# Loading half of w1 ahead of x, and a new order for the opening of a fused convolution and max-out kernel

## The chip, the cores and the metric

The kernel runs on one core of a Trainium2 chip. A core has five engines that run side by side, each in the order of its own instruction list: TensorE (PE in the profile; its weight loads stand apart as PEld), VectorE (DVE), ScalarE (ACT), GpSimd (POOL) and SyncE (SP, which here only starts transfers). They wait for each other by semaphores. The metric is device time of one execution in microseconds. Three runs of the kernel before took 405.36, 405.75 and 405.82 us; the median is 405.75.

## The reference

Two stages. First a convolution whose weights are a softmax of an input: for every token, head and tap (8 heads, 7 taps), `w = softmax(weight_gen)` over the taps, and the output is the sum over the 7 latest tokens of `w * x`. Then a max-out layer on all 33280 tokens of width 192:

```
h1 = x @ w1        # 192 x 1024
h2 = x @ w2
out = maximum(h1, h2) @ w_out   # 1024 x 192
```

## The kernel before

**The algebra.** `max(h1, h2) = h1 + relu(h2 - h1)`, so the kernel needs `wd = w2 - w1` (bf16) for the hidden products, a relu, `w_out`, and a small product `w10 = w1 @ w_out` that gives the `h1` part straight from the convolved x. `wd` has six blocks of 512 features: blocks 0 and 1 are the first 128 rows of w2 - w1 for the two halves of the features, block 2 the last 64 rows of both halves; blocks 3, 4 and 5 are the same with the two halves of the partitions swapped, made on PE with a shifted identity (`turn`, into `turned` in PSUM) and copied out by ACT (`turn_out`).

**The tiling.** Tokens lie as 128 partitions by 260 columns. Columns come in batches of 16, a batch in units: four of 4 columns in the first two batches (units 0 to 7), 8 columns from then on. A unit's path: ACT takes exp of the weights (`exp_sum`, line 153), DVE sums over the taps (`red`, line 168), ACT takes the log (`ln`, line 172), DVE subtracts it (`shift`, line 177), ACT takes exp again into `en_t` (`weights`, line 191), DVE multiplies with seven shifted copies of x into `m_t` (`mul`, line 211). In units 0 to 7 PE sums the taps and transposes in one go with identity products (`sum_transpose`, line 281), and ACT copies the sum out (`sums_out`, line 293); from unit 8 on DVE adds the taps (lines 227 to 236) and a transposing DMA on SP brings the result to `yt`. Then PE makes the hidden tiles (line 336), ACT the relus (line 346), PE the output products (lines 376 and 388), ACT copies the results out (`evac`, line 434) and SP stores them.

**What sets the order.** The opening, to about 47 us, is a list of steps written out by hand, `OPENING` (line 721). Each step is a letter and its numbers; the program emits the steps' instructions one after the other, so that each engine gets its own share of them in this order. An `@step` behind a load makes its trigger wait for the end of that other step. The letters:

```
lg.b  load the weights of batch b (SP for b < 2, else POOL)    xf  load the first columns of x (SP)
lw.h.w  load half h of the first 128 rows of w1 (w=0) or w2 (w=1)   lt.h.w  half h of the last 64 rows
lx.b.o.n  load n columns of x in bf16 (POOL)   lo  load w_out (POOL)   lh  copy the halo
xa, xv  cast x on ACT, on DVE    X exp   n sum over taps   l log   s subtract   W exp into en_t   m multiply
c.i  cast block i of w1 (ACT)   d.i  block i of wd (DVE)   t.i  turn it (PE)   T.i  copy the turned block (ACT)
v, V  transpose w1 on PE, copy it (ACT)   p, C  product w10 (PE), copy it (ACT)   k.n  n idle products that keep PE busy
y, e  sum and transpose (PE), copy it (ACT)   h hidden tile (PE)   r relu (ACT)
A, B, D  first and second half of the output products (PE; B is a wait on ACT)   E  copy the results (ACT)
```

The loads of SP use eight semaphores in turn, so that the ninth load waits for the landing of the first, the tenth for the second, and so on. After the opening a loop over groups of three hidden tiles runs to the end; the softmax steps of later batches stand at fixed places in it (`SOFTMAX_AT`, line 744), in ACT's list. The last result of all is copied from two PSUM banks by one ACT instruction into `o_last` and stored by two transfers, one from ACT's queue and one from SP's (line 422).

Of the kernel before, what the change touches and what calls it, by code (L numbers as in the profile page):

```python
# [17 lines left out]
def _sub(base: bass.AP, off: int, dims):  # L18
    ap = [list(base.ap[0])] + [[int(s), int(c)] for s, c in dims]
    return dataclasses.replace(base, offset=base.offset + off, ap=ap)  # L20
# [3 lines left out]
def kernel(  # L24
# [9 lines left out]
    nc = tc.nc  # L34

    B, S, D = x.shape
# [17 lines left out]
    def dcol(c):  # L54

        return (c + ROT) % CPP
# [292 lines left out]
    def column(c):  # L349

        for u, (b, o, n) in enumerate(UNITS):
            k = c - BATCHES[b][0] - o
            if 0 <= k < n:
                return u, k // 2, k % 2

    def place(p):

        u, i, _ = column(2 * p)
        b, o, n = UNITS[u]
        return BATCHES[b][0] + o + i, n // 2  # L360
# [55 lines left out]
    def evac(p, n):  # L416

        tile_, at = op_at[p]
        o = o_t[0]
        if p == NT // 2 - 1:  # L420

            nc.scalar.copy(out=_sub(o_last, 0, [[D, 2], [1, D]]),
                           in_=_sub(tile_, at, [[512, 2], [1, D]]))
            for j, eng in enumerate((nc.scalar, nc.sync)):
                eng.dma_start(
                    out=bass.AP(tensor=out.tensor, offset=dcol(place(p)[0] + 2 * j) * D, ap=[[CPP * D, P], [1, D]]),
                    in_=o_last[:, j * D:(j + 1) * D],
                )
            return
        runs = [[q for q in range(p, p + n) if column(2 * q)[0] == u]  # L430
                for u in range(column(2 * p)[0], column(2 * (p + n - 1))[0] + 1)]
        for qs in runs:
            c, h = place(qs[0])
            copied = nc.scalar.copy(out=_sub(o, c % 24 * D, [[D, len(qs)], [h * D, 2], [1, D]]),  # L434
                           in_=_sub(tile_, at + (qs[0] - p) * D, [[D, len(qs)], [512, 2], [1, D]]))
        stores = []
        for q in range(p, p + n):
            u, i, _ = column(2 * q)
            if u == NU - 2 and UNITS[u][2] == 8 and i % 2:
                stores.append((nc.sync, place(q)[0] - 1, [4 * D, 2], [1, 2 * D]))  # L440
            elif u < NU - 1 and i == UNITS[u][2] // 2 - 1:
                w = i + 1
                for k in range(0, 2 * w, w if u in PARTED else 2 * w):
                    stores.append((nc.sync, place(q)[0] - i + k, [1, (w if u in PARTED else 2 * w) * D]))
            if u == NU - 1:
                stores.append((nc.sync, place(q)[0], [2 * D, 2], [1, D]))
        for eng, c, *ap in stores:

            def issue(eng=eng, c=c, ap=ap, o=o):
                eng.dma_start(  # L450
                    out=bass.AP(tensor=out.tensor, offset=dcol(c) * D, ap=[[CPP * D, P], *ap]),
                    in_=_sub(o, c % 24 * D, ap),
                )

            if 3 <= u < NU - 3:
                held.append(issue)
            else:
                while u > 3 and held:
                    held.pop(0)()
                issue()  # L460
        return copied
# [8 lines left out]
    OUTS, c = [[], [], []], 0  # L470
    for g in range(3, len(GROUPS)):
        most = 4 if g == 3 else 2 if GROUPS[g][1] == 2 or len(OUTS[-1]) == 4 else 4
        n = min(most, ready[g] - c)
# [21 lines left out]
    def hidden(g, now=(), between=lambda: None, beside=lambda: None, ahead=lambda: None,  # L495
               before=lambda: None, after=lambda: None):


        t0, n = GROUPS[g]
        rd = room(g)  # L500
        for t in range(t0, t0 + n - 1):
            hid_tile(t)
        if now:
            out_room(now, "a" if n == 1 and "a" in ps else None)
            last = out_first(now)
        for t in range(t0, t0 + n - 1):
            relu(rd, t, 1)
        go = relay(last) if now else None
        hid_tile(t0 + n - 1)
        before()  # L510
        if len(now) > 2:
            beside()
        relu(rd, t0 + n - 1, 1)
        ahead()
        if now:
            out_second(now, go)
            evac(now[0] // 2, len(now) // 2)
        between()
        after()
        if len(now) <= 2:  # L520
            beside()

    def rest_of_results(c):

        parts = [p for p in (c[:4], c[4:-2], c[-2:]) if p]
        assert max(map(len, parts)) <= 4
        go = []
        for i, now in enumerate(parts):
            out_room(now, ("r", "a", "c")[i])
            go.append(relay(out_first(now)))  # L530
            if i:
                out_second(parts[i - 1], go[i - 1])
                evac(parts[i - 1][0] // 2, len(parts[i - 1]) // 2)
        out_second(parts[-1], go[-1])
        evac(parts[-1][0] // 2, len(parts[-1]) // 2)
# [10 lines left out]
    o_last = consts.tile([P, 2 * D], FP32, name="o_last")  # L546
# [155 lines left out]
    def results_buffer(_):  # L702
# [16 lines left out]
    }  # L719

    OPENING = """
        lg.0 xf.-6.6 xf.0.4 lt.1.0 lt.0.0 k.2 lw.0.1 k.19 lw.0.0 lt.1.1 lw.1.0 lt.0.1 X.0.0.2 k.1 n.0.0.2
        X.0.1.2 lw.1.1 k.1 k.2 n.0.1.2 l.0.0.2 s.0.0.2 xa.-6.4 l.0.1.2 W.0.0.0 lx.0.4.4@l.0.0.2 lg.1 xv.-2.6
        W.0.0.1 s.0.1.2 W.0.12 c.0 lx.0.12.4@W.0.12 W.0.8 m.0.0.0 m.0.0.1 W.0.4 y.0.0 y.0.1 c.2 e.0.0 c.1
        e.0.1 d.0 d.2 t.0 k.3 t.2 T.3 d.1 T.4 h.0 h.1 t.1 X.1 r.0 lx.0.8.4 T.1 lo.0 r.1 m.0.4 n.1 v.0 h.2
        lx.1.0.8 V.1 y.1 r.2 l.1 h.3 e.1 m.0.8 lg.2@l.1 s.1 V.0 m.0.12 r.3 h.4 W.1.0 m.1.0 y.2 h.5 r.4 p.0
        e.2 r.5 h.6 lx.1.8.8@r.4 lg.3@e.2 y.3 W.1.8 h.7 lh.2 C.1 C.0 C.2 A.3 W.1.4 X.2 r.6 e.3 B.3 m.1.4 h.8
        D.3 y.4 r.7 r.8 Z.0 E.3 n.2 X.3 l.2 m.1.8 A.4 e.4 W.1.12 lx.2.0.8.0@r.7 B.4 h.9 D.4 h.10 r.9 E.4 s.2
        r.10 lg.4@r.9 y.5 W.2.0 A.5 h.11 B.5 h.12 e.5 D.5 n.3 r.11 r.12 A.6 m.1.12 E.5 h.13 B.6 D.6 y.6 r.13
        E.6 h.14 e.6 l.3 lx.2.8.8@r.13 h.15 r.14 A.7 W.2.8 B.7 y.7 D.7 r.15 e.7 E.7  # L730
    """

    make_identity(nc, ident_f)
# [91 lines left out]
```

## Time and profile before

| | |
|---|---|
| median of 3 runs | 405.75 us |
| the profiled execution | 405.37 us, of which the span is 403.6 us |
| PE busy | 394.8 us, 98% of the span |
| DVE busy | 369.1 us, 91% |
| ACT busy | 360.9 us, 89% |
| DMA | 63.16 MB moved, mean 157 GB/s |
| granted TensorE clock | 1.00 throughout |

The span runs from the first instruction of the program to the last; the 1.8 us between it and the execution's time lie around it. In the timeline a row has the start and the length in microseconds, then engine, line, operation, and what it writes and reads. A stretch in which nothing on the longest chain runs is shown as "issue". The landing of a transfer is given in the views of a tile as the time from its issue to its landing.

### The profile page before, as it was taken

The numbers are of one execution on the slowest core, as the hardware profiler recorded it, in microseconds if no ns is written. First come the engines' busy times: TensorE is split into PE (matmuls) and PEld (weight loads), VectorE is DVE, ScalarE is ACT, GpSimd is POOL, SyncE is SP. The second block draws the span as 40 slices with busy tenths as digits, with TensorE's granted clock in tenths as the row PEclk, the third lists the DMA queues.
The fourth block names the chain that finished last, engine by engine and source line by source line (L and its number), as shares of the span: only waits on it lengthen the run. The fifth ranks groups of instructions, "written<-read, shape, count | busy, mean of one in ns | idle before, by whom it ended". The sixth has DMA issues, their size and how long they took to land.

```text
span 403.6 us, 16321 instructions
## 1 busy us (share of the span) xinstructions
PE 394.8 (98%) x7499; PEld 321.3 (80%) x7499; DVE 369.1 (91%) x211; ACT 360.9 (89%) x466; POOL 72.3 (18%) x96
## 2 busy tenths in 40 slices
PE   7799999999999999999999999999999999999996
PEld 3589999777778777778777778877777877787996
DVE  5999999999999999999999999999999999998200
ACT  5999899999999989999899999989999899888872
POOL 3111031211122210222220122122012121200000
PEclk9999999999999999999999999999999999999999
DMA  8956468767768646864766667777457847558304
GB/s 262 222 140 151 120 124 167 183 164 133 190 110 222 182 79 129 240 187 80 217 187 107 141 192 193 99 215 198 81 115 228 178 80 200 141 106 193 104 31 169
DMA packets 60883, 63.16 MB, mean 157 GB/s; under 512 B 47641, under 2 KB 48665, under 8 KB 60816
## 3 DMA queue, kind: packets, MB, share of 16 engines
q1 hardware_dynamic: 52816, 40.15, 36.4%
q0 software_dynamic: 7856, 21.89, 27.4%
q8 instruction: 58, 0.95, 1.0%
q10 hardware_dynamic: 144, 0.10, 0.1%
q14 instruction: 9, 0.07, 0.1%
HBM read 36.55 MB, written 25.56 MB: 154 GB/s over the span
## 4 chain that ended last, share of the span: by engine, by line
PE 92%; ACT 5%; DMA 1%; SPq 1%; issue 0%
PE op_ps L376 42%; PE hdc L336 13%; PE hdb L336 13%; PE hda L336 13%; PE op_ps L388 8%; ACT rd_t L346 2%; DMA ws0E<-in_moe_w_dram 1%; PE hdp L336 1%; PE yps L281 1%; ACT en_t L191 1%; ACT yt L293 1%; ACT e_t L153 0%; ACT w1t L644 0%; SPq L574 0%; ACT w L622 0%
## 5 line engine op out<-in xcount | busy, mean ns | idle before, releaser
L376 PE MATMUL op_ps<-wo,rd_t 64*128 64x192 bf16 x4160 | 210.6, 243 | 0.0
L376 PEld LDWEIGHTS <-rd_t 64*128 64x128 bf16 x4160 | 181.0, 94 | 14.7
L211 DVE TENSOR_TENSOR m_t<-xb,en_t 128x10752 bf16<-128x10752 bf16 (+2 forms) x39 | 187.8, 4821 | 1.5 <-ACT en_t L191 1.4
L336 PEld LDWEIGHTS <-wd 64*128 64x128 bf16 x1824 | 96.8, 94 | 40.4 <-issue 2.5
L346 ACT ACTIVATE rd_t<-hdc 128x1024 bf16<-128x1024 f32 x82 | 84.1, 1025 | 17.8 <-PE hdc L336 16.2
L253 POOL CAST gate<-yt 128x1 f32<-128x1 bf16 x30 | 39.9, 1332 | 271.3 <-DMA yt<-y_t 271.3
L346 ACT ACTIVATE rd_t<-hda 128x1024 bf16<-128x1024 f32 x81 | 83.4, 1030 | 0.2 <-ACT o_t L434 0.2
L346 ACT ACTIVATE rd_t<-hdb 128x1024 bf16<-128x1024 f32 x81 | 83.5, 1031 | 0.0
L227 DVE TENSOR_TENSOR m_t<-m_t 128x4608 bf16<-128x4608 bf16 (+1 forms) x30 | 73.0, 2433 | 0.1
L336 PE MATMUL hdc<-yt,wd 64*128 64x512 bf16 (+1 forms) x552 | 67.9, 353 | 0.0
L434 ACT COPY o_t<-op_ps 128x384 f32<-128x384 f32 (+1 forms) x99 | 56.1, 577 | 12.4 <-PE op_ps L376 12.3
L336 PE MATMUL hdb<-yt,wd 64*128 64x512 bf16 (+1 forms) x540 | 67.1, 355 | 0.0
L336 PE MATMUL hda<-yt,wd 64*128 64x512 bf16 (+1 forms) x540 | 67.1, 355 | 0.0
L388 PE MATMUL op_ps<-w,yt 64*128 64x192 bf16 x780 | 55.5, 243 | 0.0
L388 PEld LDWEIGHTS <-yt 64*128 64x128 bf16 x780 | 39.0, 94 | 14.5 <-issue 0.3
L233 DVE TENSOR_TENSOR m_t<-m_t 128x3072 bf16<-128x3072 bf16 (+1 forms) x30 | 50.2, 1674 | 0.1
L191 ACT ACTIVATE en_t<-wg_t 128x896 bf16<-128x896 f32 (+3 forms) x48 | 35.7, 773 | 3.0 <-PE op_ps L376 2.0
L236 DVE TENSOR_TENSOR y_t<-m_t 128x1536 bf16<-128x1536 bf16 (+1 forms) x30 | 27.5, 916 | 0.6
L177 DVE TENSOR_TENSOR wg_t<-wg_t,sum_t 128x280 f32<-128x280 f32 (+6 forms) x46 | 22.2, 483 | 0.0
L168 DVE TENSOR_REDUCE sum_t<-e_t 128x64 f32<-128x448 f32 (+3 forms) x31 | 19.7, 639 | 2.3 <-ACT e_t L153 2.3
L125 POOL DMA_DIRECT2D xb<-in_x_dram x34 | 18.2, 537 | 17.3 <-ACT rd_t L346 11.0
L153 ACT ACTIVATE e_t<-wg_t 128x896 f32<-128x896 f32 (+2 forms) x18 | 15.9, 886 | 2.1 <-DMA wg_t<-in_weight_gen_dram 2.1
(40 smaller groups left out, 110.0 us busy)
## 6 DMA issues: line engine op xcount, KB each, us to landing
out_dram<-o_t SPq DMA_DIRECT2D x21, 768.0 KB, 4.3
xb<-in_x_dram POOLq DMA_DIRECT2D x30, 384.0 KB, 5.0
out_dram<-o_t SPq DMA_DIRECT2D x22, 384.0 KB, 3.7
wg_t<-in_weight_gen_dram POOLq DMA_DIRECT2D x13, 448.0 KB, 5.7
xb<-xb POOLq DMA_DIRECT2D x7, 288.0 KB, 5.1
wg_t<-in_weight_gen_dram SPq DMA_DIRECT2D x2, 448.0 KB, 5.2
xb<-in_x_dram POOLq DMA_DIRECT2D x4, 192.0 KB, 6.4
xs<-in_x_dram SPq DMA_DIRECT2D x1, 576.0 KB, 4.3
```

The costliest lines, as they stand in the source:

```text
L177: nc.vector.tensor_tensor(out=w_t, in0=w_t, in1=_sub(s_ts[b], hs.start, [[1, hs.stop - hs.start], [0, K]]), op=ALU.subtract)
L191: act = nc.scalar.activation(out=_sub(en_ts[b], (o * WGC + ((i or 0) * J + j) * N * K) * 2, [[2 * N, K], [2, N], [1, 2]]), in_=_sub(wg_ts[ ...
L211: return nc.vector.tensor_tensor(out=m_out, in0=x_in, in1=_sub(en_ts[b], at * H * 2, [[2, K * n * H], [0, G // 2], [1, 2]]), op=ALU.mult,)
L227: nc.vector.tensor_tensor(out=taps(0, 1, 3), in0=taps(0, 1, 3), in1=taps(3, 1, 3), op=ALU.add)
L233: nc.vector.tensor_tensor(out=taps(0, 2, 2), in0=taps(0, 2, 2), in1=taps(1, 5, 2), op=ALU.add)
L236: nc.vector.tensor_tensor(out=_sub(y_ts[b], o * D, [[64, 2], [P, 3 * w // 2], [1, 64]]), in0=taps(0, 1, 1), in1=taps(2, 1, 1), op=ALU.add,)
L253: nc.gpsimd.tensor_copy(out=gate, in_=yt[:, 0:1])
L336: nc.tensor.matmul(hid_out(t, f, j), lhsT=wd_at(j, s, f // 4, f % 4 * P, P), rhs=_sub(yt_ts[u][half(j), :], (s + j) % 3 * P, [[3 * P, w // ...
L346: relu_of[t0] = nc.scalar.activation(out=rd[:, k * 1024:(k + n) * 1024], in_=hd[:, at:at + n * 1024], func=AF.Relu)
L376: return nc.tensor.matmul(op_out(c), lhsT=rd[rows, k * 1024 + at:k * 1024 + at + P], rhs=wo[rows, f * D:(f + 1) * D], start=False, stop=(r ...
L388: nc.tensor.matmul(op_out(c + j), lhsT=yt_ts[u][half(j), (3 * i + (s + j) % 3) * P:(3 * i + (s + j) % 3 + 1) * P], rhs=w10[half(j), s * D: ...
L434: copied = nc.scalar.copy(out=_sub(o, c % 24 * D, [[D, len(qs)], [h * D, 2], [1, D]]), in_=_sub(tile_, at + (qs[0] - p) * D, [[D, len(qs)] ...
```

## The change

Three things change; the rest of the program is the same, and every step of the opening is still there.

1. The list `OPENING` is written in another order. On SP's queue the first half of the first 128 rows of w1 (`lw.0.0`) is loaded ahead of x instead of sixth in the weights; the last rows (`lt`) come ahead of the second halves; the first rows of w2 come last before `lg.1`. On DVE both `n`, then both `s`, come ahead of the cast of x, and `d.2` ahead of `d.0`. On ACT both `l` come ahead of `xa`, `c.0` right behind it, `W.0.8` and `W.0.4` ahead of `W.0.0.1`, and the order of the casts, copies and relus differs up to `e.7`. On PE all but one of the 28 idle products stand ahead of the first `y` (25 before), and `t.1` comes ahead of `h.0` instead of behind `h.1`.
2. Some triggers wait for other steps: `lx.0.4.4` for `l.0.1.2`, `lx.0.12.4` for nothing of its own, `lx.0.8.4` for `W.0.12`, `lo` for `e.0.0`, `lg.3` for `r.3` (and it now stands ahead of `lx.1.8.8`, which waits for `W.1.0`).
3. The last copy is split: ACT copies the one half of `o_last`, DVE the other, each followed by its store. In the built program DVE's copy waits for the semaphore of ACT's copy.

```diff
@@ -419,9 +419,8 @@
-            nc.scalar.copy(out=_sub(o_last, 0, [[D, 2], [1, D]]),
-                           in_=_sub(tile_, at, [[512, 2], [1, D]]))
-            for j, eng in enumerate((nc.scalar, nc.sync)):
+            for j, (eng, copy) in enumerate(((nc.scalar, nc.scalar.copy), (nc.sync, nc.vector.tensor_copy))):
+                copy(out=o_last[:, j * D:(j + 1) * D], in_=tile_[:, at + 512 * j:at + 512 * j + D])
                 eng.dma_start(
@@ -719,15 +718,15 @@
     OPENING = """
-        lg.0 xf.-6.6 xf.0.4 lt.1.0 lt.0.0 k.2 lw.0.1 k.19 lw.0.0 lt.1.1 lw.1.0 lt.0.1 X.0.0.2 k.1 n.0.0.2
-        X.0.1.2 lw.1.1 k.1 k.2 n.0.1.2 l.0.0.2 s.0.0.2 xa.-6.4 l.0.1.2 W.0.0.0 lx.0.4.4@l.0.0.2 lg.1 xv.-2.6
-        W.0.0.1 s.0.1.2 W.0.12 c.0 lx.0.12.4@W.0.12 W.0.8 m.0.0.0 m.0.0.1 W.0.4 y.0.0 y.0.1 c.2 e.0.0 c.1
-        e.0.1 d.0 d.2 t.0 k.3 t.2 T.3 d.1 T.4 h.0 h.1 t.1 X.1 r.0 lx.0.8.4 T.1 lo.0 r.1 m.0.4 n.1 v.0 h.2
-        lx.1.0.8 V.1 y.1 r.2 l.1 h.3 e.1 m.0.8 lg.2@l.1 s.1 V.0 m.0.12 r.3 h.4 W.1.0 m.1.0 y.2 h.5 r.4 p.0
-        e.2 r.5 h.6 lx.1.8.8@r.4 lg.3@e.2 y.3 W.1.8 h.7 lh.2 C.1 C.0 C.2 A.3 W.1.4 X.2 r.6 e.3 B.3 m.1.4 h.8
-        D.3 y.4 r.7 r.8 Z.0 E.3 n.2 X.3 l.2 m.1.8 A.4 e.4 W.1.12 lx.2.0.8.0@r.7 B.4 h.9 D.4 h.10 r.9 E.4 s.2
-        r.10 lg.4@r.9 y.5 W.2.0 A.5 h.11 B.5 h.12 e.5 D.5 n.3 r.11 r.12 A.6 m.1.12 E.5 h.13 B.6 D.6 y.6 r.13
-        E.6 h.14 e.6 l.3 lx.2.8.8@r.13 h.15 r.14 A.7 W.2.8 B.7 y.7 D.7 r.15 e.7 E.7
+        lg.0 lw.0.0 xf.-6.6 xf.0.4 X.0.0.2 n.0.0.2 lt.1.1 lt.1.0 lt.0.0 X.0.1.2 lw.1.0 lt.0.1 n.0.1.2
+        l.0.1.2 l.0.0.2 k.2 s.0.1.2 xa.-6.4 lw.0.1 s.0.0.2 c.0 lw.1.1 k.3 lx.0.4.4@l.0.1.2 lg.1 W.0.0.0
+        xv.-2.6 W.0.8 W.0.4 W.0.0.1 k.1 W.0.12 lx.0.12.4 m.0.0.0 k.19 m.0.0.1 k.2 d.2 y.0.0 y.0.1 d.0 c.1
+        t.0 lx.0.8.4@W.0.12 e.0.0 e.0.1 lo.0@e.0.0 t.2 c.2 T.4 k.1 T.3 d.1 t.1 h.0 h.1 X.1 r.0 T.1 h.2 m.0.4
+        y.1 n.1 m.0.8 v.0 r.1 l.1 r.2 e.1 lx.1.0.8 V.1 s.1 V.0 m.0.12 h.3 r.3 h.4 lg.2@l.1 W.1.0 m.1.0 y.2
+        h.5 lg.3@r.3 p.0 r.4 r.5 h.6 lx.1.8.8@W.1.0 h.7 lh.2 e.2 C.0 W.1.4 C.2 C.1 y.3 r.6 A.3 W.1.8 m.1.4
+        X.2 B.3 h.8 e.3 D.3 y.4 W.1.12 Z.0 r.7 E.3 r.8 A.4 h.9 X.3 m.1.8 n.2 lx.2.0.8.0@W.1.12 B.4 e.4 l.2
+        h.10 D.4 s.2 lg.4@l.2 y.5 r.9 E.4 A.5 h.11 r.10 B.5 D.5 e.5 r.11 h.12 W.2.0 n.3 m.1.12 A.6 E.5 h.13
+        B.6 D.6 y.6 r.12 E.6 r.13 l.3 e.6 lx.2.8.8@r.12 W.2.8 A.7 h.14 r.14 h.15 B.7 r.15 y.7 D.7 e.7 E.7
     """
```

## The prediction

> **What bounds the kernel now.** I read the page's busy times and slices first, then the chain of waits up to 33 us, then the timelines of DVE, ACT, PE and the queues where the change sits.
>
> ```profile
> span 403.6 us, 16321 instructions
> PE 394.8 (98%) x7499; PEld 321.3 (80%) x7499; DVE 369.1 (91%) x211; ACT 360.9 (89%) x466; POOL 72.3 (18%) x96
> PE   7799999999999999999999999999999999999996
> DVE  5999999999999999999999999999999999998200
> PEclk9999999999999999999999999999999999999999
> ```
>
> PE is full from the third slice to the last, at full clock. So the change can alter only how early PE becomes full, whether it later starves, and the last microseconds. The chain, with columns start, length, what:
>
> ```profile
> 3.98 5.95 DMA ws0E<-in_moe_w_dram
> 9.95 0.03 ACT w L622
> ...
> 14.54 0.95 ACT e_t L153
> 15.49 0.91 ACT rd_t L346
> ...
> 28.28 1.03 ACT rd_t L346
> 29.36 0.83 PE hdp L336 x12
> ```
>
> A load carries the chain to 9.95, ACT to 29.3, PE from there to 400. The timeline of the instructions that the forecast rests on:
>
> ```profile
> 5.94 0.71 POOL L125 DMA_DIRECT2D xb<-in_x_dram  x1 [3.64 <-ACT sum_t L172]
> 7.43 0.37 SPq L118 DMA_DIRECT2D wg_t<-in_weight_gen_dram  x1
> 9.25 1.07 POOL L125 DMA_DIRECT2D xb<-in_x_dram  x2 [2.60 <-ACT en_t L191]
> 14.54 0.95 ACT L153 ACTIVATE e_t<-wg_t 128x896 f32<-128x896 f32 x1
> 20.38 0.83 PE L336 MATMUL hdp<-yt,wd 64*128 64x256 bf16 x12 [0.82 <-ACT yt L293]
> 34.19 1.08 DVE L177 TENSOR_TENSOR wg_t<-wg_t,sum_t 128x896 f32<-128x896 f32 x1
> 84.64 0.31 ACT L172 ACTIVATE sum_t<-sum_t 128x128 f32<-128x128 f32 x1
> 88.48 0.43 PE L388 MATMUL op_ps<-w,yt 64*128 64x192 bf16 x6
> 400.56 0.34 SPq L425 DMA_DIRECT2D out_dram<-o_last  x1
> ```
>
> `lg.1`, issued at 7.43, lands 7.1 later, at 14.52, and `X.1` (14.54) starts on it at once. PE has 4.66 us of idle pieces after 9.5 us. The largest are 1.04 ahead of 20.38, 0.86 between the two first `y`, and 0.59 ahead of 29.36; behind that only 0.24, at 79.66. A second chain is nearly as tight: DVE needs 11.85 us a unit against PE's 11.3 and eats up its lead, so the transposed `yt` of units 30 and 32 lands only 1.57 and 1.66 us before PE uses it.
>
> **The change part by part.**
>
> *Loads of SP.* Landings follow the order of issue, across SP's and POOL's queues together. `lw.0.0` now stands ahead of x; two neighbouring loads land 0.65 to 0.88 apart (7.41 to 8.01 for half the partitions, 8.01 to 8.68 for all). x therefore lands some 0.65 later: 6.15 and 7.0 to 7.45 instead of 5.49 and 6.81. DVE does both `s` in that time; its cast of x (0.76) starts at 7.36 or so, and the first product at 8.2 instead of 8.11: +0.1 on DVE. `lw.0.0` lands near 5.3 instead of 9.93, so the chain's first wait (9.95) goes. ACT then finishes its early exps and first casts at about 10.4 instead of 11.77. Little of that 1.3 us lasts: `T.3` and `T.4` still wait for DVE's `d` and PE, and `X.1` for `lg.1`, which is late next.
>
> *Idle products.* Two more ahead of the first `y` (27 for 25) are 2 x 0.2145, the duration of a warm one: +0.43, `y.0.0` at 10.14 instead of 9.72. ACT's copies and `d.0` behind it leave room, since `h.0` waits for `T.3` and `T.4` (idle 0.60, 0.43 and 0.43 at 13.0 to 14.6). Nothing; 0.43 if that cover is gone.
>
> *`t.1` ahead of `h.0`.* It waits for `d.1`, hence for the last half of w1 (`ws1E`, landed 13.07). DVE's subtraction is 0.69, so `t.1` at 13.85 or later, and `h.0` behind it. It still ends before `r.0` can run behind `X.1` (15.4). Nothing, but each 0.1 by which that load lands after 13.6 would count in full. Its issue moves ahead of `lx.0.4.4`'s, which speaks for 12.2 to 12.6.
>
> *`lg.1`, the main unknown.* Its issue waits for the landing of the second x load (7.0 to 7.45), so 7.4 to 7.8. The second x trigger of POOL no longer waits for `W.0.12`: it comes right behind the first, which starts 0.3 after `l.0.1.2` ends (6.17), at 6.48; 0.71 and 0.54 make 7.65. So the two are in a tie. If `lg.1` goes first, it has the same bytes ahead of it as before, and `X.1` starts when ACT is through, at 14.1 to 14.5 (-0.4 to 0). If `lx.0.12.4` goes first, `lg.1` has that transfer's place: before, `lx.0.12.4` landed at 15.08 with those bytes ahead of it (+0.56). Should both POOL loads fall ahead with gaps, 15.4 to 15.6. I take 14.9, nearer the tie's late side because POOL's order is fixed and SP's waits: x = +0.4. From 14.54 to 29.3 the chain lies almost wholly on ACT, and DVE's `n.1` reads what `X.1` writes, so x passes on to both.
>
> The row that decides this: `lx.0.4.4` was issued at 5.94, between SP loads of 5.60 and 6.83, and landed at 12.88, between theirs (11.90, 13.07). [...]
>
> *POOL's later triggers.* `lx.0.8.4`, now behind all of `W.0.12`, goes at 10.7 instead of 9.77; with its 7.2 to landing, 17.9. `m.0.8` reads it and began at 17.63 before, now at 17.63 + x = 18.0: nothing, bounds 0 and 0.3 if it lands at 18.3. `lo` and `lx.1.0.8` follow, 1.6 later than before, landing near 20.4 and 22.2; PE first reads w_out at 27.3 and DVE those columns at 24.4: nothing. `lg.2`, `lg.3` and `lx.1.8.8` move by under 2 us, with more than that to their readers: nothing.
>
> *ACT and PE up to 29 us.* `h.2` and `y.1` come ahead of `V`, and `e.1` behind two relus: the idle 1.04 ahead of 20.38 and most of the 0.59 ahead of 29.36 go, against the 0.43 above and up to 0.69 for `t.1`. PE alone is 0.2 to 0.5 early, before x. Bounds: -0.9 (below, as a rival) and 0.
>
> *DVE behind 30 us.* `n.2` now follows `m.1.8`, and on ACT `W.1.12` (two pieces, 0.60) and `e.4` (0.69) stand ahead of `l.2`, which ran at 33.23: 34.5, so `s.2` at 34.9 instead of 34.19, +0.7. Then `W.2.0` has moved behind `e.5` and `r.11`. On ACT, from 34.5: 0.22 + `r.9` 0.93 + `E.4` 0.38 + `r.10` 1.02 + a wait for `y.5` of 0.25 + `e.5` 0.75 + `r.11` 0.95 + `W.2.0` 1.05 = 40.1. DVE is ready for `m.2.0` at 39.77 and started it before at 36.19 + 2.87 = 39.06. Lag 1.1, plus x. From here DVE never idles, so the lag stays. It meets PE in the list of ACT: at 84.64 a `ln` comes 0.82 after DVE's reduce (83.20 + 0.62 = 83.82) and was not waiting. Now it waits 1.1 + x - 0.82 = 0.28 + x. The relus and the copy of results behind it (87.67 + 0.47 = 88.14) are late by that, and PE's use of that bank (88.48) had 0.34 to spare: end +0.28 + x - 0.34 = x - 0.06. If `e.4` or PE's part run 0.3 earlier than laid here, the lag is 0.8 and this term only x - 0.36.
>
> *The tail.* ACT's copy of 0.48 becomes a half, 0.31 (the row of a 64x192 copy, line 667, is 0.31), and DVE's half waits for it: 0.33 to 0.38 (DVE rows of 168 and 224 elements). Store of SP at 400.05 + 0.31 + 0.35 + 0.05 = 400.75 instead of 400.56; it lands 1.86 after issue, ACT's 2.02, so the end moves from 402.58 to about 402.62: +0.05, bounds -0.1 (the copies overlap) and +0.15.
>
> *Sum.* 0.4 - 0.06 + 0.05 = +0.4. The profiled execution took 405.37 (span 403.6 and 1.8 around it), 0.38 below the median; I take the same shift for both, so +0.4 on 405.75: 406.15, given as 406.2.
>
> **The rivals.**
>
> R1, forecast: `lg.1` at 14.7 to 15.0, 406.2 (own range 405.9 to 406.6). For it: the tie of 7.4 to 7.8 against 7.65.
>
> R2: `lg.1` stays ahead of `lx.0.12.4`, x = 0: 405.75 - 0.06 + 0.05 = 405.7. For it: SP's issue may be at 7.4. [...]
>
> R3, faster: DVE's lag stays under 0.8 and does not bind, and PE keeps what it saves: -1.04 - 0.59 + 0.69 + 0.05 = -0.89: 404.85. For it: ACT is 1.3 us ahead at 10.4, and the chain to 29 us is ACT's. Against it: `X.1` waits on `lg.1`, in the middle of it.
>
> R4, slower, the other side of no change: `lg.1` behind both x loads and the half-partition loads, 15.4 to 15.6: x = 0.9 to 1.1, +1.0 - 0.06 + 0.05 and 0.2 because a DVE lag of 2.1 also exceeds the slack of units 30 and 32 (1.57, 1.66) part of the time: 406.95. It decides from a landing at 15.2. For it: 128 KB in 64 partitions cost nearly as much time (0.60) as 256 KB.
>
> **How the numbers follow.** R1 0.40, R2 0.16, R3 0.17, R4 0.27. 0.2% is 0.8 us, about what a measurement of this kernel can tell from no change. Slower by more: R4 and the upper end of R1, 0.27 + 0.08 = 0.35. Faster by more: R3, 0.17, less a little for its upper half, 0.15. The rest, 0.50, is within. The range for 8 in 10 runs from R3's middle, 404.9, to just above R4's, 407.1.
>
> **What would show it.** Right: `X.1` (ACT, line 153, 896 elements) at 14.7 to 15.0 on the landing of `lg.1`; the shift of 896 elements at 34.9 + x; the product behind at 40 + x; a `ln` near 85 waiting for DVE's reduce; DVE's last copy behind ACT's. Wrong: `X.1` at 14.2, or later than 15.2; no wait of ACT on DVE near 85; a PE idle of over 0.5 behind 30 us; `t.1` waiting past 14.2 for `d.1`.

## The result: slower, by 2.5 us

The changed kernel takes 408.24 us (median of 9, 406.81 to 411.25) against 405.74 of before (405.36 to 406.58): a ratio of 1.0067, 95% interval 1.0043 to 1.0092. A second series gave 408.32 against 405.55, 1.0075 (1.0057 to 1.0093). The forecast was 406.2 with a range to 407.1. Two things stand out: the time itself, and its spread, 4.4 us where that of before is 1.2. (A long execution is not the changed kernel's alone: of 104 executions of the kernel before in all series nine took 407.1 to 409.3; none of the nine was profiled.)

The head of the page of the profiled execution (408.61 us), the totals and PE's slices:

```profile
span 406.8 us, 16321 instructions
PE 396.1 (97%) x7499; PEld 321.9 (79%) x7499; DVE 369.7 (91%) x212; ACT 361.0 (89%) x466; POOL 68.2 (17%) x96
PE   7799899999999999999999999999999999999996
```

The span is 3.2 longer and PE's work 1.3 longer; all its slices have the digits of before but the fifth (41 to 51 us), which has fallen from 9 to 8. The chain of waits of the changed kernel, up to 19 us:

```profile
1.66 0.42 SPq L557
2.08 0.04 issue
2.12 6.66 DMA xs<-in_x_dram
8.79 0.02 issue
8.80 7.16 DMA wg_t<-in_weight_gen_dram
15.97 0.02 issue
15.99 0.95 ACT e_t L153
16.94 0.91 ACT rd_t L346
```

The chain is no longer the load of w1 that it was before. It is x, then `lg.1`: the second x load takes 6.66 us and lands at 8.79 (6.81 before), `lg.1` waits for that landing on SP's queue, is issued at 8.80 and takes 7.16 as it did before (7.1). So `X.1` starts at 15.99 instead of 14.54. The timeline of the rows that answer to those of the forecast:

```profile
8.80 0.33 SPq L118 DMA_DIRECT2D wg_t<-in_weight_gen_dram  x1
9.74 3.03 DVE L211 TENSOR_TENSOR m_t<-xb,en_t 128x2688 bf16<-128x2688 bf16 x2
36.39 1.09 DVE L177 TENSOR_TENSOR wg_t<-wg_t,sum_t 128x896 f32<-128x896 f32 x1 [1.24 <-ACT sum_t L172]
41.73 5.76 DVE L211 TENSOR_TENSOR m_t<-xb,en_t 128x10752 bf16<-128x10752 bf16 x1 [0.38 <-ACT en_t L191]
49.49 0.47 PE L281 MATMUL yps<-around,m_t 64*128 64x64 bf16 x20 [1.95 <-issue]
87.96 0.31 ACT L172 ACTIVATE sum_t<-sum_t 128x128 f32<-128x128 f32 x1
403.73 0.36 DVE L423 COPY o_last<-op_ps 128x192 f32<-128x192 f32 x1 [24.14 <-ACT o_last L423]
404.11 0.34 SPq L424 DMA_DIRECT2D out_dram<-o_last  x1
```

The first product starts at 9.74 instead of 8.11, and PE's first sum 1.6 later than before. And at 47.37 PE stops for 2.12 us in the middle of one sum, after 64 of its 84 products, with nothing to wait for ("issue"); it resumes at 49.49. (Idle pieces of PE are counted here as in the prediction, from one product's start plus the usual spacing to the next one's start; the bracket in a row has the shorter gap behind the modelled end, here 1.95.) Its idle pieces behind 9.5 us come to 6.80 against 4.66. The later start of the sums (1.64) and that stop (2.12), less the 0.43 of idle products that moved ahead, are about the 3.2 us of this execution. All four signs of being wrong that the prediction gave are there: `X.1` later than 15.2, this stop, no wait of ACT on DVE near 85 (the logarithm at 87.96), and `t.1` at 14.67, waiting past 14.2 for `d.1`.

### The profile page after: what moved, and what is told of

Read it like the earlier page. It is cut to its first block, busy times and chain, and to the rows that moved or that the text cites. A ratio compares the mean times of both kernels' runs of the same rounds, so it can differ in the third digit from the quotient of the medians.

```text
span 406.8 us, 16321 instructions
## 1 busy us (share of the span) xinstructions
PE 396.1 (97%) x7499; PEld 321.9 (79%) x7499; DVE 369.7 (91%) x212; ACT 361.0 (89%) x466; POOL 68.2 (17%) x96
## 4 chain that ended last, share of the span: by engine, by line
PE 94%; DMA 3%; ACT 1%; issue 1%; SPq 0%; DVE 0%
PE op_ps L376 42%; PE hdc L336 13%; PE hdb L336 13%; PE hda L336 13%; PE op_ps L388 8%; PE hdp L336 2%; PE yps L281 2%; DMA wg_t<-in_weight_gen_dram 2%; DMA xs<-in_x_dram 2%; PE pw L657 0%; ACT rd_t L346 0%; ACT e_t L153 0%; ACT o_t L433 0%; PE tp L638 0%; ACT en_t L191 0%
## 5 line engine op out<-in xcount | busy, mean ns | idle before, releaser
L253 POOL CAST gate<-yt 128x1 f32<-128x1 bf16 x30 | 35.7, 1189 | 277.9 <-DMA yt<-y_t 277.9
```

The costliest lines, as they stand in the source:

```text
L253: nc.gpsimd.tensor_copy(out=gate, in_=yt[:, 0:1])
```

## The experiments

All times are compared with the kernel before on the same chip. Where a diff shows the order, it has the tokens that move.

### Once more, and one change alone

The changed kernel unchanged:

> The changed kernel once more, unchanged. Theory (two causes that belong to the program: the second x load lands about 1.7 us later than laid out, at 8.79; and PE stands 2.12 us at 47.4 because a 16 KB fetch of its instructions waits behind a load of x columns): this profile shows x landing at 8.5 to 9.0 and a PE idle of 1.5 to 2.5 us near 47 again, time 407.5 to 409. Rival (both were accidents of the one profiled execution): x lands at 7.0 to 7.6, no PE idle over 0.5 us behind 30 us, and the times spread between 406 and 409.

It took 408.32 (407.32 to 410.02). The profile has x at 8.51, a stop of PE of 0.83 at 47.01, and again nothing else over 0.5 behind 30 us. Both places belong to the program; the length of the stop varies.

The kernel before, with that half of w1 moved ahead of x and nothing else:

```diff
-        lg.0 xf.-6.6 xf.0.4 lt.1.0 lt.0.0 k.2 lw.0.1 k.19 lw.0.0 lt.1.1
+        lg.0 lw.0.0 xf.-6.6 xf.0.4 lt.1.0 lt.0.0 k.2 lw.0.1 k.19 lt.1.1
```

> The kernel before with nothing but the first half of w1 moved from seventh on SP's queue to second, ahead of x. Theory: x lands 1.5 to 2 later, the first product starts at 9.6 to 9.8, PE's first sum 1.6 later, and since PE has no idle to make it up with: +1.3 to +1.6, 407.2. By the prediction's own step: x 0.65 later, the first product at 8.8 (the order of DVE is not changed here), +0.7, 406.4.

407.42 against 405.55, 1.0055 (1.0040 to 1.0069). x landed at 8.79. DVE's cast of x, in the kernel before and then in this one:

```profile
6.90 0.76 DVE L700 CAST xb<-xs 128x1152 bf16<-128x1152 f32 x1 [0.50 <-DMA xs<-in_x_dram]
```

```profile
8.89 0.76 DVE L700 CAST xb<-xs 128x1152 bf16<-128x1152 f32 x1 [2.36 <-DMA xs<-in_x_dram]
```

This one move brings 1.9 us, a little over the 1.3 to 1.6 of the theory and far from the 0.7 of the prediction's step; the four of its six runs with a mean clock of 0.998 or more have a median of 407.16, +1.6. Is it the bytes? The same with a load of half the size:

```diff
-        lg.0 xf.-6.6 xf.0.4 lt.1.0 lt.0.0
+        lg.0 lt.1.0 xf.-6.6 xf.0.4 lt.0.0
```

> The kernel before with a load of half the partitions (the last rows lt.1.0, 128 KB) moved ahead of x instead of the 256 KB of the first half of w1. Theory (what stands ahead of x delays it by more than its interval later in the queue, in proportion to its bytes): x lands at 7.7 to 8.2 instead of 6.8 to 7.0, +0.8 to +1.1 on the time, 406.4. Rival by the prediction's intervals (0.6 to 0.65 a load whatever its size): x at 7.4 to 7.6, 406.1. Rival (only the loads of full rows of w1 are slow ahead of x): x at 7.0 to 7.2, 405.6.

It took 408.64, 1.0075 (1.0050 to 1.0099), and every number expected was too low: half the bytes delay x as much, in one profile each. The timeline of this kernel on SP, DVE and PE:

```profile
1.19 0.56 SPq L574 DMA_DIRECT2D ws0T<-in_moe_w_dram  x1
1.81 1.04 SPq L558 DMA_DIRECT2D xs<-in_x_dram  x2
8.86 0.76 DVE L700 CAST xb<-xs 128x1152 bf16<-128x1152 f32 x1 [2.26 <-DMA xs<-in_x_dram]
11.68 0.79 PE L281 MATMUL yps<-around,m_t 64*128 64x64 bf16 x42 [1.73 <-DVE m_t L211]
```

Its windows (columns: stretch, its length, busy time of PE, PEld, DVE, ACT and POOL with counts, granted clock, DMA share, GB/s):

```profile
12.00:14.00 2.00, 1.32 (x66) 1.20 (x59) 2.00 (x3) 2.00 (x7) 1.72 (x3) 0.79 1.10 317
14.00:16.00 2.00, 2.00 (x22) 0.88 (x17) 1.79 (x3) 0.95 (x2) 0.00 (x0) 0.50 1.12 255
16.00:18.00 2.00, 1.33 (x9) 0.32 (x9) 2.00 (x1) 1.26 (x3) 0.00 (x0) 0.85 1.44 193
```

x lands at 8.77, and DVE has stood 2.26 us for it. Part of both delays is SP's issue: the second x load is issued at 1.65 in the kernel before, at 2.12 behind the half of w1 and at 2.42 behind the small load, and takes 5.16, 6.67 and 6.35 from there to its landing. PE idled 1.89 ahead of its first sum, and its clock then was at half for 3.41 us (13.17 to 16.58). So a late x cost twice here: the wait, and in some executions a slow clock behind it. Seven profiles with any load ahead of x have its landing at 8.5 to 9.7 us; in ten with x right behind `lg.0` it is at 6.8 to 7.7; the medians are 8.79 and 7.14.

### The clock

Five more idle products ahead of the first sum of the changed kernel:

```diff
-        d.2 y.0.0 y.0.1
+        d.2 k.5 y.0.0 y.0.1
```

> The changed kernel with five more idle products ahead of the first sum, 5 x 0.2145 = 1.07 us of PE work, which fit in the idle of 1.16 to 1.36 us there. Theory (in the executions with a mean clock of 0.992 to 0.996, PE stood too long ahead of the first sum and ran at a reduced clock for some microseconds behind it): the clock is 0.999 to 1.00 in nearly all runs, and the times lie at 406.8 to 408.2 with a median near 407.4. Rival (the low clock has nothing to do with that idle): 5 of 9 runs still at 0.992 to 0.996, median 408.2 or more.

The clock came out as expected: a mean of 0.999 or 1.00 in all six runs, where nine of the fifteen runs of the changed kernel had 0.992 to 0.996. The time did not: 408.54 (407.27 to 409.45). In its profile x landed at 9.70, later than in any other, and PE waited for it at a granted clock of 1.00 (8 to 12 us). The clock is a part of the spread, not the cause of the loss: of the changed kernel's fifteen runs the six at 0.998 or more have a median of 407.60, the nine others of 408.75, and both are slower than before.

The kept traces show where the clock fell. In every profile the idle products start 0.43 apart at first and 0.21 apart from some moment between 5.16 and 8.55 on, which is the moment at which the record of a full clock begins (5.85 in the kernel before, 8.24 in the changed one, so it was not 1.00 throughout). In both of these the record stays at full for 399.36 us, 117 times 3.41, and falls behind the end of the span, at 405.21 and 407.60. While the program ran it fell in four profiles, and stayed at half for 3.41 us in three of them and for twice that in one, that of the kernel `x_first` below (columns as above). Counted in periods of 3.41 us from the start of the full clock, each fall stood at the end of a period; PE was idle in these four for 1.86, 1.90, 2.18 and 2.41 us in all, by the modelled ends, and no period with 1.78 or less was followed by a fall. The windows of `x_first`:

```profile
12.00:16.00 4.00, 3.17 (x87) 2.25 (x88) 4.00 (x5) 2.49 (x7) 1.98 (x3) 0.61 1.01 240
16.00:20.00 4.00, 3.92 (x30) 1.92 (x30) 4.00 (x3) 3.50 (x6) 0.00 (x0) 0.54 1.22 156
```

So in these profiles the falls went with the idle time within one period, and where the periods lay differed from execution to execution. That is how nearly the same idle could be followed by a slow clock in one execution and not in the next. A period at half speed costs up to 1.7 us, an estimate from its length of 3.41 and from the idle products, 0.43 apart before the full clock and 0.21 in it.

### The stop of PE at 47 us

In the changed kernel, the load of x columns that is in flight then (`lx.2.8.8`, 384 KB, triggered by POOL) is made to wait longer:

```diff
-        e.6 lx.2.8.8@r.12 W.2.8
+        e.6 lx.2.8.8@e.6 W.2.8
```

> The changed kernel with one trigger later: the load of x columns that was in flight at 44.5 to 47.7 waits for e.6 instead of r.12, about 2.4 us later, so that the fetch of PE's instructions that is due near 44.2 finds the queues free. Theory: the idle of 2.12 at 47.4 is gone; DVE's lag, which it hid, takes back 0.4 at the logarithm near 86, so -1.7: 406.5 at the same landing of x. Rival (the stall moves to the next fetch, or is not due to that load): a PE idle of over 1 us somewhere between 44 and 60 remains, 407.7 or more.

The stop is gone: no PE idle over 0.5 behind 30 us. But the time is 408.02, not 406.5. In this profile x landed at 9.51 and PE idled 2.45 ahead of the first sum, with a clock of 0.58 from 12 to 16 us; so the term is not refuted by the total, nor shown by it. (All six runs have a mean clock of 0.992 to 0.996; less one period at half speed, up to 1.7, the total would be near the 406.5 expected. This is an estimate.) The reverse experiment shows it. The kernel before, with the wait of the changed kernel at this one load:

```diff
-        l.3 lx.2.8.8@r.13 h.15
+        l.3 lx.2.8.8@r.12 h.15
```

> The kernel before with one trigger earlier: the load of x columns near 42.7 waits for r.12 instead of r.13, as in the changed kernel, so it is issued at about 40.85, beside the store of 40.93 instead of 1.7 behind it. Theory (the 16 KB fetch of PE's instructions that starts right behind the landing of that store finds the queues taken by this load when it is issued less than about 1.2 behind the store): the fetch starts 1.5 to 3 later than 43.4, PE idles 0.5 to 2.2 us between 43 and 47, and the time is 0.5 to 2.2 above 405.5, more where the clock falls behind the idle. Rival (the stall belongs to the late phase of the changed kernel, not to this trigger): no idle, 405.5.

407.39 (407.12 to 408.26), 1.0037 (1.0026 to 1.0049): a token of the order, +1.7 us. Its profile (408.26) has a second such stop, of 0.89 at 65.6. Its timeline, then its DMA queues between 44 and 46 us and between 46.0 and 47.1 (packets, MB, share of the engines):

```profile
41.02 0.54 POOL L125 DMA_DIRECT2D xb<-in_x_dram  x1 [4.21 <-ACT rd_t L346]
41.12 0.34 SPq L450 DMA_DIRECT2D out_dram<-o_t  x1
48.22 0.47 PE L281 MATMUL yps<-around,m_t 64*128 64x64 bf16 x20 [1.51 <-issue]
```

```profile
q0 software_dynamic: 107, 0.29, 84.1%
```

```profile
q8 instruction: 1, 0.02, 5.5%
```

The kernel before, on the same rows, then its queues between 43.3 and 44.5:

```profile
40.93 0.34 SPq L450 DMA_DIRECT2D out_dram<-o_t  x1
42.66 0.53 POOL L125 DMA_DIRECT2D xb<-in_x_dram  x1 [6.05 <-ACT rd_t L346]
```

```profile
q0 software_dynamic: 18, 0.06, 53.4%
q8 instruction: 1, 0.02, 5.4%
```

Before, the load is issued 1.73 behind the store, and a packet on the instruction queue starts at 43.41, as the store lands (43.43). In the experiment the load goes out with the store; the queues are 84% busy with it, there is no instruction packet from 44 to 46, it comes at 46.05, and PE, stopped at 46.53, resumes at 48.22, 2.2 behind it. The queue, named "instruction" in the profile, has 58 such packets of 16 KB in an execution, for 14,998 instructions of PE, one for each 259, so they are taken to be PE's instructions. The five profiles with a stop of 0.8 to 2.1 there have the load 0.1 ahead to 1.41 behind the store (1.21 in the changed kernel); with 1.73 or more there is none in any profile. From 1.2 to 1.5 it goes either way, and with 1.50 one profile has a stop of 0.59.

### x first, and the rest of the new order

The changed kernel with the half of w1 behind the small loads:

```diff
-        lg.0 lw.0.0 xf.-6.6 xf.0.4
+        lg.0 xf.-6.6 xf.0.4
...
-        lt.1.1 lt.1.0 lt.0.0 X.0.1.2
+        lt.1.1 lt.1.0 lt.0.0 lw.0.0 X.0.1.2
```

> The changed kernel with the half of w1 put back behind the three small loads, so that x is loaded right behind the weights again. Theory: x lands near 6.8, the first product starts near 8.1 instead of 9.74, lg.1 lands near 14.5 and X.1 starts at 14.1 to 14.6; -1.5 us against the changed kernel where the fetch of instructions stalls as before, about 406.7. Rival (x is late for another reason, such as the bytes of lt and the second halves in flight): x still lands after 8.3 and the time stays at 408.2.

408.80 (408.11 to 409.79), and neither theory: x landed at 7.36, but the first product started at 10.44. On ACT the cast `c.0` stands ahead of all exps into `en_t`, and now it waited for the load behind it, 2.10 us. The row of ACT:

```profile
9.40 0.62 ACT L621 CAST w<-ws0E 128x512 bf16<-128x512 f32 x1 [2.10 <-DMA ws0E<-in_moe_w_dram]
```

The edit was incomplete. It shows that the new order of ACT needs its new order of loads. With the cast behind `W.0.12` as well:

```diff
-        s.0.0.2 c.0 lw.1.1
+        s.0.0.2 lw.1.1
...
-        k.1 W.0.12 lx.0.12.4
+        k.1 W.0.12 c.0 lx.0.12.4
```

> The changed kernel with the half of w1 behind the three small loads of last rows, and its cast c.0 behind W.0.12, so that ACT does not stand at that cast with the exps behind it. All the rest of the new order stays. Theory (the late x is the main cost of the change, with the clock that falls behind the longer idle of PE): x lands at 6.8 to 7.4, the first product starts at 8.1 to 8.5, PE idles under 0.6 us ahead of its first sum, granted clock 1.00; 405.6 to 406.3. Rival (the rest of the order costs as much by itself, through DVE's lag and the stall near 47): over 407.

Inconclusive by its median of 408.60, with times from 406.06 to 411.69. The profile (409.7) has x at 7.38, the first product at 8.34, 0.21 of idle ahead of the first sum, clock 1.00 there: the first cause is gone. The second is there in full, a stop of PE of 2.07 at 46.82, and this time the clock fell behind it. Its windows, columns as above:

```profile
47.00:49.00 2.00, 0.10 (x8) 0.10 (x8) 2.00 (x2) 0.71 (x1) 0.00 (x0) 1.00 0.00 0
49.00:51.00 2.00, 2.00 (x47) 1.87 (x46) 2.00 (x3) 1.27 (x2) 0.00 (x0) 0.69 0.03 8
51.00:53.00 2.00, 2.00 (x25) 1.82 (x22) 2.00 (x3) 1.27 (x2) 0.00 (x0) 0.50 0.49 197
```

The clock was at half from 49.76 to 53.17, which by the estimate above costs up to 1.7 more than the stop. The stop of 2.12 in the changed kernel's own profile lay across two periods of 3.41 us, with 1.65 of idle in the one, and had no fall behind it; here 1.86 us of idle lay within one.

Then the same with the old order from the step behind `E.3` on (near 33 us), which also puts `l.2` and `n.2` early and that load back behind `r.13`:

```diff
-        X.2 B.3 h.8 e.3 D.3 y.4 W.1.12 Z.0 r.7 E.3 r.8 A.4 h.9 X.3 m.1.8 n.2 lx.2.0.8.0@W.1.12 B.4 e.4 l.2
+        X.2 B.3 h.8 e.3 D.3 y.4 Z.0 r.7 E.3 r.8 n.2 X.3 l.2 m.1.8 A.4 e.4 W.1.12 lx.2.0.8.0@r.7 B.4 h.9
...
-        e.5 r.11 h.12 W.2.0 n.3
...
+        y.5 W.2.0 A.5 h.11 B.5 h.12 e.5 D.5 n.3 r.11 r.12
...
-        lx.2.8.8@r.12 W.2.8
+        lx.2.8.8@r.13 h.15 r.14 A.7 W.2.8
```

> As the kernel with x first and the cast moved, and from the step behind E.3 on (near 33 us) the order of before: n.2 ahead of m.1.8, l.2 ahead of e.4 and W.1.12, W.2.0 ahead of e.5 and r.11, the x columns behind r.13. Theory: no lag of DVE at the logarithm near 85, no stall of PE near 47; 0.3 to 0.6 under the kernel with x first and the cast moved, 405.0 to 405.7, and so not slower than before. Rival: the late part of the order is neutral, and this one equals it within 0.2.

406.62 (405.78 to 411.09), 1.0044 (1.0015 to 1.0073): better, not yet 405.7. PE has no stop, but idles 1.53 at 15.94, because `lg.1` landed at 15.53. With the wait of `lx.0.12.4` put back:

```diff
-        c.0 lx.0.12.4 m.0.0.0
+        c.0 lx.0.12.4@W.0.12 m.0.0.0
```

> The kernel with x first, the cast moved and the old order behind E.3, with the wait of lx.0.12.4 for W.0.12 put back, as before. Theory (lg.1 lands at 15.4 to 15.5 there because this load of x columns is issued ahead of it, and X.1, r.0 and h.2 wait for it, PE idle 1.5 at 15.9): lg.1 lands at 14.3 to 14.7, X.1 starts by 14.8, the idle at 15.9 falls to 0.7 or less, and the time by 0.7 to 1.0, to 405.6 to 405.9. Rival (lg.1 is late by its own issue): it lands after 15.2 again, 406.5.

`X.1` of the kernel without the wait, then of the one with it, from their timelines on ACT:

```profile
15.55 0.95 ACT L153 ACTIVATE e_t<-wg_t 128x896 f32<-128x896 f32 x1 [0.93 <-DMA wg_t<-in_weight_gen_dram]
```

```profile
14.24 0.96 ACT L153 ACTIVATE e_t<-wg_t 128x896 f32<-128x896 f32 x1
```

`lg.1` was issued at 7.57 and 7.61. With the second load of x columns ahead of it, it took 8.0 to land, without it 6.6. The three profiles with x first and without that wait have its landing at 15.09 to 15.53, the three with it at 13.86 to 14.31. The median did not fall, 406.64 against 405.71, 1.0018 (1.0001 to 1.0035), but the times now lie in two groups: 405.37 to 406.19 in six runs, 407.10 to 408.40 in the other six. The profile, of 407.33, has a stop of PE of 1.96 at 46.25, with the load 1.41 behind the store. If that is the second group, it goes away when the load waits one step longer:

```diff
-        l.3 lx.2.8.8@r.13 h.15
+        l.3 lx.2.8.8@l.3 h.15
```

> The kernel with x first, the cast moved, the old order behind E.3 and lx.0.12.4 gated, and besides the load of x columns near 42.4 made to wait for l.3, about 1 us later, so 2.4 or more behind the store. Theory (the two groups of times of the gated kernel, 405.4 to 405.7 and 407.1 to 408.4, differ by the fetch of PE's instructions that does or does not get through ahead of this load): one group only, 405.3 to 405.9, no PE idle near 46, not slower than before. Rival (the second group has another cause): two groups again, median over 406.3.

One group, 404.90 to 405.91, median 405.38 against 405.59: 0.9981 (0.9960 to 1.0001). The sum near 46 us in the profiles of the two kernels, first the one with the two groups, then this one; all 84 products now run in one piece, with 0.32 of idle in it:

```profile
45.83 0.60 PE L281 MATMUL yps<-around,m_t 64*128 64x64 bf16 x29
48.21 0.47 PE L281 MATMUL yps<-around,m_t 64*128 64x64 bf16 x20 [1.78 <-issue]
```

```profile
45.02 1.72 PE L281 MATMUL yps<-around,m_t 64*128 64x64 bf16 x84
```

It is the best of the study, as fast as before or a little faster; its interval just reaches 1.

### DVE's lag, the middle, the tail, and x by itself

The whole new order with the three causes undone. It differs from the last kernel by the part of the order behind `E.3`: `l.2`, `n.2` and `W.2.0` are late again, and with them relus, copies and three triggers stand elsewhere:

```diff
-        lg.0 lw.0.0 xf.-6.6 xf.0.4
+        lg.0 xf.-6.6 xf.0.4
...
-        k.1 W.0.12 lx.0.12.4 m.0.0.0
+        k.1 W.0.12 c.0 lx.0.12.4@W.0.12 m.0.0.0
...
-        e.6 lx.2.8.8@r.12 W.2.8
+        e.6 lx.2.8.8@e.6 W.2.8
```

> The whole new order of the changed kernel with three things undone: the half of w1 behind the three small loads with its cast behind W.0.12, the wait of lx.0.12.4 for W.0.12, and the load of x columns waiting for e.6 instead of r.12. Against the kernel with the old order behind E.3 it differs by l.2, n.2 and W.2.0 alone, DVE's lag. By the prediction's step (the logarithm near 85 waits for DVE, which has lost about 1.1): ACT waits there, PE idles 0.3 to 0.5 near 88, and it is 0.2 to 0.8 slower than that kernel: 405.8 to 406.4. Rival (the lag is hidden): equal within 0.2.

405.75 against 405.59, 0.9995 (0.9981 to 1.0009), and 0.37 above the kernel with the old late order, where the eleven times of each overlap. Its timeline:

```profile
84.57 0.61 DVE L168 TENSOR_REDUCE sum_t<-e_t 128x64 f32<-128x448 f32 x1
85.21 0.31 ACT L172 ACTIVATE sum_t<-sum_t 128x128 f32<-128x128 f32 x1 [0.61 <-DVE sum_t L168]
88.68 0.42 PE L388 MATMUL op_ps<-w,yt 64*128 64x192 bf16 x6 [0.15 <-ACT o_t L433]
```

ACT stands 0.61 at that logarithm, and PE, three microseconds on, 0.42 in all ahead of 88.68: the prediction's chain from DVE through ACT to PE, in the place that it named. In the changed kernel's own profile (87.96, no wait) the 2.12 us stop had hidden it: of the profiles with this late order the five without a stop of PE have a wait of 0.29 to 0.61 there, the three with one have none.

The kernel before with the new order from `r.0` to `E.3` alone:

```diff
-        X.1 r.0 lx.0.8.4 T.1 lo.0 r.1 m.0.4 n.1 v.0 h.2 lx.1.0.8 V.1 y.1 r.2 l.1 h.3 e.1 m.0.8
+        X.1 r.0 lx.0.8.4 T.1 lo.0 h.2 m.0.4 y.1 n.1 m.0.8 v.0 r.1 l.1 r.2 e.1 lx.1.0.8 V.1 s.1
...
```

> The kernel before with the changed kernel's order from r.0 to E.3 alone (16 to 33 us: h.2 and y.1 ahead of the transposes of w1, e.1 behind two relus, the casts and weights between), the old order ahead of it and behind it. By the prediction's step (the idle of 1.04 ahead of 20.38 and the 0.59 ahead of 29.36 go, nothing else is late): 404.0 to 405.1, DVE no later than before; this would be the part of the change that gains. Rival (the two idles only move, since the next relu or the transposed sum is late instead): 405.3 to 405.9.

406.24 (405.33 to 407.94), 1.0014 (0.9998 to 1.0029). The rival is nearer: the idles of 1.04 and 0.59 are gone, and others are there. From its timeline:

```profile
16.98 0.28 PE L336 MATMUL hdp<-yt,wd 64*128 64x256 bf16 x2 [0.41 <-ACT rd_t L346]
37.00 0.42 PE L388 MATMUL op_ps<-w,yt 64*128 64x192 bf16 x6 [0.22 <-ACT o_t L434]
```

`h.2`, earlier now, waits 0.59 for the relu `r.0`; 0.40 more are lost at 36.6 and 0.28 at 39.4, and 0.59 at 46.8, where the load is 1.5 behind the store.

The split tail alone, the opening of before:

```diff
-            nc.scalar.copy(out=_sub(o_last, 0, [[D, 2], [1, D]]),
-                           in_=_sub(tile_, at, [[512, 2], [1, D]]))
-            for j, eng in enumerate((nc.scalar, nc.sync)):
+            for j, (eng, copy) in enumerate(((nc.scalar, nc.scalar.copy), (nc.sync, nc.vector.tensor_copy))):
+                copy(out=o_last[:, j * D:(j + 1) * D], in_=tile_[:, at + 512 * j:at + 512 * j + D])
```

> The opening of before with the split last copy. By the prediction's term: +0.05 (bounds -0.1 and +0.15), 405.6 to 405.7 against 405.55 in the last comparison. Rival (the split is what spreads the changed kernel's times): 406.5 or more, or a spread of over 1.5 us.

405.43 against 405.50, 0.9998 (0.9987 to 1.0008): nothing, as its term said.

Last, the changed kernel with x late as it is, but at full clock and without the stop:

```diff
-        d.2 y.0.0 y.0.1
+        d.2 k.5 y.0.0 y.0.1
...
-        e.6 lx.2.8.8@r.12 W.2.8
+        e.6 lx.2.8.8@e.6 W.2.8
```

> The changed kernel with x late as it is, but with five more idle products ahead of the first sum (no clock loss there) and the load of x columns waiting for e.6 instead of r.12 (no stall of PE near 47). What is left is the late x with what follows from it, lg.1 and X.1 1.4 to 2.5 late, and DVE's lag. Theory: one group of times, 407.2 to 408.0, clock 0.999 to 1.00 in all runs; x alone is then worth about 2 of the changed kernel's 2.7. Rival (x's landing is made up for later): under 406.7.

407.22 (406.69 to 408.86) against 405.59, 1.0035 (1.0016 to 1.0054), clock 0.998 to 1.00. The late x with all that follows from it is worth 1.6 us, DVE's lag in it; the stop and the clock make the other 1.0 or so, by the difference of two series, and the wide spread. Removed one at a time they brought -0.3 and +0.2, each in six runs, so how the 1.0 is shared between them is not shown.

## Why the prediction was wrong

*Wrong: what a load costs ahead of x.* The step "two neighbouring loads land 0.65 to 0.88 apart", hence x 0.65 later, first product at 8.2. Measured: x 1.7 to 2.9 later than in the profile of before, 1.65 by the medians, and the product at 9.74. The distances that the step quotes are 0.60 and 0.67, between landings deep in a full queue, and there the trace of before has others too: two more loads of 256 KB land 1.25 and 1.19 behind their neighbours (8.68 to 9.93, 10.41 to 11.60). At the head of the queue even 128 KB moved the landing as much as 256 KB. The packets of the traces show part of how: x's packets start 0.9 later behind the half of w1 (4.21 against 3.28), and while in the kernel before the 16 DMA engines end the first x load within 0.43 us of each other and the second within 0.76 (6.05 to 6.81), in the changed kernel they end 0.69 and 1.72 apart (7.07 to 8.79), so that the last lands late. In the profile with the small load ahead there is also a microsecond in which only 5 to 13 engines work. Why the engines drift apart is not settled.

*Wrong: what else waits for that landing.* "Its issue waits for the landing of the second x load" was right, and with x at 8.79 it gave 15.97 instead of 14.9. The tie with POOL's second load was never played there, since that load was issued by 8.10. R4's mechanism, `lg.1` behind that load, is real all the same: in the kernels with x first it costs 1.3 (15.55 against 14.24). R2's order of issue came true there as well: `lg.1` was issued at 7.57 to 7.87, and in the three profiles in which DVE's cast of x runs while POOL issues its second load, that issue took 0.98 to 1.10 instead of 0.55 and ended 0.12 behind the cast, at 8.1 to 8.4. But `lg.1` landed at 15.09 or later all the same.

*Missing: the fetch of PE's instructions.* Of POOL's later triggers the forecast said that they "move by under 2 us, with more than that to their readers: nothing". It looked at who reads the loaded columns, and did not price `lx.2.8.8` behind `r.12` at all. Who else uses the DMA queues at that moment was the question; the answer was worth up to 2.1 us, and by the estimate above up to 1.7 more where the clock fell.

*Missing: the clock.* The granted clock of 1.00 in all slices was read as a fact of the kernel. In the profiles it stayed at 1.00 behind every period of 3.41 us with up to 1.78 of idle and fell behind the four with 1.86 to 2.41, and the forecast put no price on such an idle; in nine of the changed kernel's fifteen runs the mean clock was lower.

*Right in kind and size.* The tail (+0.05, measured none). DVE's lag: the shift was put at 34.9 + x and the product behind at 40 + x; with x = 1.45 that is 36.35 and 41.5, measured 36.39 and 41.73. With x at nought its price came out at 0.37 where the likeliest case had -0.06 and the term without PE's slack 0.28; the kernels compared differ by more than the lag alone. R3's gain was not there: PE's two idles go, as said, but 1.27 of others come in their place, with the half of w1 where it was.

The forecast's 406.2 is close to what the new order would cost with x, `lg.1` and the columns left alone (405.75). The first load made the larger part of the difference, 1.6 us; the stop and the clock made the rest.

## What to carry to other kernels

The distance of two landings in a full queue was not the price of putting one ahead of the load that everything waits for; here a load of either size moved the landing by 1.65 to 2 us, about three times that distance. Follow every trigger that waits for that landing. When a trigger moves, ask who else needs the DMA queues then, PE's instruction fetch among them: here a PE idle put down to "issue" in the middle of a run of matmuls (1.95 of a stop of 2.12 in the changed kernel) was its mark, and one wait more on the load cured it. Where times spread by microseconds, look for a cause of two outcomes before averaging, for it may be one that can be removed.

## What the runs showed of the hardware that was not expected

- In five profiles PE stopped for 0.8 to 2.1 us while a 16 KB packet of the queue "instruction" (58 in an execution, one for each 259 instructions of PE) came late, with a 384 KB load issued 0.1 ahead of a store to 1.41 behind it. The packet then started 1.4 to 2.6 us behind the store's landing (47.19 and 44.58 in the changed kernel), elsewhere within 0.5 of it (43.41 and 43.43 in the kernel before), and PE resumed 2.2 to 2.4 us behind its start (49.49 in the changed kernel). In the profile with the stop of 0.59 it started in time, and PE resumed 2.9 behind it.
- The granted clock of PE was recorded at full for 399.36 us, 117 periods of 3.41, in the kernel before and in the changed one, from 5.85 and 8.24 on (5.16 to 8.55 over all profiles). It fell to half behind four periods with 1.86 to 2.41 us of idle in all, for one period in three profiles and two in one, and behind none with 1.78 or less.
- A trigger of POOL took 0.98 to 1.10 us instead of 0.55 where DVE cast x meanwhile, and ended 0.12 behind the cast (three profiles).
- A load of 128 KB ahead of x delayed its landing as much as one of 256 KB (8.77 and 8.79, where before has 6.81), 0.77 and 0.47 of it by SP's later issue.
